# Weight conversion: low words rounded by ScalarE and added by GpSimd, the range test by TensorE, and new planner positions

## The chip, the cores and the metric

The kernel runs on one core of one Trainium2 chip. The metric is the device time of one execution in microseconds, the median of several runs. The core has five engines that run side by side, each working through its own queue in order: TensorE (PE in the profile, its weight loads PEld), VectorE (DVE), ScalarE (ACT), GpSimd (POOL) and SyncE (SP), which here issues nearly all DMAs.

## The reference

An attention block without softmax feeds a two-layer network:

```python
kv = np.einsum('bhsd,bhse->bhde', k, v)          # q, k, v: (8, 8, 576, 64) float32
out = np.einsum('bhsd,bhde->bhse', q, kv)
rms = np.sqrt(np.mean(out * out, axis=-1, keepdims=True) + 1e-06)
attn = (out / rms * g_norm).astype(np.float32)
x = attn.transpose(0, 2, 1, 3).reshape(4608, 512)
h = x @ w_in                                      # (512, 2048)
g = np.maximum(h, 0.0) + np.log1p(np.exp(-np.abs(h)))
return (g @ w_out).astype(np.float32)             # (2048, 512)
```

w_in and w_out are float64: every weight arrives as two 32-bit words, and the kernel makes a float32 of them before anything else.

## The kernel before

**Precision.** The large products run as three float32r matmuls each: an operand is split into a high part, a low part and a third part (high minus 4096 times low), in `split_weight` for weights and in `split` for x. Each split is a chain over ACT and DVE.

**Weights.** There are 16 chunks c of 128 of the 2048 inner columns. Operand j = 2c is the chunk of w_in, j = 2c + 1 that of w_out; each is 128 x 512 float64, 512 KB, fetched by SP into the buffer `raw` (`rawb` for odd j of the first eight chunks). Each of the two buffers has one place, so the next fetch into it waits for everything that reads the one before. `weight(j, ...)` then converts, for every operand:

- ACT `square` (L434) squares the exponent part of the high word, for a test of the weight's range;
- DVE `high1` (L438) and `high2` (L442) shift the bits of the high word, and the top three bits of the low word's share, into float32 form;
- DVE `mask` (L447) sets weights that are too small to zero;
- ACT `beyond` (L451) sums over the squares into a column of `over`, which shows weights that are too large; `whole_scale` adds up `over` late in the kernel and makes of it the factor `scale` of the last output stage;
- DVE `power` (L455) takes the weight's power of two, `rest` (L460) multiplies it with the low word, and `total` (L464) adds the two: the rounded float32.

The result goes into `split_weight`. For the first eight operands (chunks 0 to 3) the third part is made on PE, by two matmuls (L525, L526, `less_by_pe`); for the others on DVE.

**Attention.** Batch b needs its kv: five groups of matmuls (`kv_of`, L696), four of loads of 256 KB of k and of v and one of tails of 128 KB, then a copy by ACT (L704). Tile t is 128 rows of x. For a tile, q is loaded and turned (L776 on PE, copy L783, for the first tiles), then come `out_rows` (L720 on PE), the square by ACT (L793), its sum by DVE (L724), the root by GpSimd (L727, L728), the scaling by DVE (L732, `norm`), and for the first twelve tiles a turn by PE (L738), the split (ACT L640, DVE L643 and L646) and a copy and a store of x (L802, L803). Two tiles are under way at a time: the buffers for the squares, for the roots and for the rows in PSUM have two places each.

**The products.** Blocks of 384 rows (three tiles) take the chunks of their first part one by one: `mm1` (L864, twelve matmuls), softplus and split (ACT L886, L888, DVE L875, L879), and three `mm2` (L871, nine matmuls). Blocks 0 to 3 take chunks 0 to 3, the others chunks 0 to 5. The rest of the chunks runs in a wide stage over 512 rows with a scheme that saves products (L1066 and L1137), from 357 us on; x, and pieces of the result, go through DRAM in between.

**The order.** All operations are tasks with an engine, an assumed duration, what they follow, the buffers they take and give back, and a position. `Plan.order` builds the order of every queue before the program is emitted: on each engine it takes, among the tasks that could start about first, the one of the lowest position. The tables P0 to P7 hold the positions and offsets by position in the work; READY and BEGIN say from when an engine is assumed to be there. Where PE has nothing to do until the first products, the planner puts in fillers: matmuls of 128x512 whose result nobody reads (`warm`, L1237). The order is fixed in the program; on the chip an engine waits at the head of its queue.

Of the kernel before, what the change touches and what calls it, by code (L numbers as in the profile page):

```python
# [10 lines left out]
U32 = mybir.dt.uint32  # L11
BF16 = mybir.dt.bfloat16
# [48 lines left out]
class Plan:  # L61
# [5 lines left out]
    READY = {"PE": 2000, "ACT": 2500, "DVE": 4000, "POOL": 2500, "SP": 700}  # L67
# [4 lines left out]
    BEGIN = 2000  # L72
# [134 lines left out]
def kernel(  # L207
# [47 lines left out]
    P0 = [-45.94, -26.77, -11.8, 0.28, -29.91, -5.64, -2.86, 3.84, -103.4, -98.98, -69.3, -76.66, -68.5, -24.67, -23.22, -34.97, 8.15, -43.02, 7.47, 9.69, 7.18, 18.16, -12.1, 4.75, 1.0, 106.19, 31.3, 6.28, 7.19, 5.22]  # L255
    P4 = [-30.17, -6.08, 16.93, -33.9, -22.35, -28.91, -17.33, -7.12, -18.68, -2.69, 0.62, 2.73, -7.38, -1.86, 1.1, 1.72, 5.22, -13.65, 3.22, 0.88, 43.88, 43.95, -0.17, -0.32, 44.8, 40.82, -20.17, -6.56, 6.41, 10.03, -10.73, 0.23, 2.8, 0.42, -9.48, -5.03]
    P5 = [1.24, -5.69, -2.28, -3.57, 1.72, 0.53, 6.68, -5.83, 3.01, -2.95, 3.35, 1.4, -6.96, 0.27, -5.34, -2.29]
    P6 = [1.05, 6.24, 4.29, 4.08, -1.52, -2.85, 1.21, -0.34, 3.11, 3.1, -1.07, -0.73, -0.88, 9.99, 5.7, 5.69, 0.13, 0.46]
    P7 = [-23.78, -17.98, -11.85, -14.93, 0.41, 1.61, 7.35, 2.7, -25.02, -6.6, -15.2, -4.48, -2.14, 0.64, 2.93, 0.97, 4.67, 5.36, 3.33, 6.57, -10.37, 2.36, -14.11, -9.89, -7.11, 12.91, -2.89, 14.55, 12.59, 9.35]
    CONVERT, FETCH, EARLY, LATER = P0[:8], P0[8:16], P0[16:27], P0[27:]  # L260
    P1 = [49.11, 48.77, 51.0, 80.9, 122.61, 131.29, 2.87, 53.84, 71.21, 480.08, 304.47, 150.69]
    P2 = [24.08, 35.56, 23.68, 37.26, 50.08, 83.13, 74.26, 112.0, 102.25, 108.09, 139.38, -110.13, 88.34, 208.35, 423.47, -209.77, 170.15, -245.78, 423.49, 179.94, -7.53]
    P3 = [2.14, 2.48, 6.41, -16.53, 0.86, 2.79, 4.01, -16.44, 3.79, 3.96, 2.19, 1.79, 0.72, 1.35, 1.55, -1.03]
# [20 lines left out]
    big = const.tile([P, 1], F32, name="big")  # L284
    over = const.tile([P, 2 * KF], F32, name="over")
# [128 lines left out]
    def weight(j, pos, fetch_pos, behind):  # L414
# [12 lines left out]
        if wide:  # L427
            sq, t, p = (slot(n) for n in ("sq", "m", "m"))
# [25 lines left out]
            def power():  # L454
                nc.vector.tensor_scalar(out=new(p, [P, d_model], U32), in0=t.tile, scalar1=0xFF800000,  # L455
                                        scalar2=None, op0=ALU.bitwise_and)
# [816 lines left out]
```

## Time and profile before

| | |
|---|---|
| median of 3 runs | 858.36 us (858.07 to 860.5) |
| profiled execution | 858.36 us, its span 856.6 us |
| PE busy / span | 843.2 us, 98% |
| DVE, ACT, POOL busy | 704.3, 520.5, 76.0 us |
| granted TensorE clock | 1.00 |
| moved by DMA | 167.09 MB, 195 GB/s over the span |

How to read it: a busy PE is not a PE at its peak, since matmuls are pipelined and their ends are modelled; two matmuls in a row overlap in the records, so the time one takes is read from start to start. Idle time of an engine is put down to what came last before it went on. SPq is the queue of SP, the issue of DMAs. In a row like "L864 PE MATMUL banks<-units,pieces" stand the line, the engine, the operation, what is written and what is read.

### The profile page before, as it was taken

How to read it: one execution, taken by the hardware profiler on the slowest of the kernel's cores; microseconds unless marked ns; L12 is line 12 of the kernel's file. 1: busy time of each engine (PE TensorE's matmuls, PEld its weight loads, DVE VectorE, ACT ScalarE, POOL GpSimd, SP SyncE). 2: the span in 40 equal slices, each digit the busy share in tenths (PEclk: the TensorE clock that was granted, in tenths of full speed). 3: DMA queues.
4: the chain of work that ended last, by engine and by line, in shares of the span. 5: the costliest groups of instructions: out<-in, count | busy, mean ns of one | idle time of the engine just before them, and what ended most of it. 6: DMA issues, size and time to landing. Idle time of an engine off the chain costs nothing.

```text
span 856.6 us, 17087 instructions
## 1 busy us (share of the span) xinstructions
PE 843.2 (98%) x6469; PEld 754.6 (88%) x6469; DVE 704.3 (82%) x998; ACT 520.5 (61%) x980; POOL 76.0 (9%) x79
## 2 busy tenths in 40 slices
PE   8899999999999999999999999999999999999998
PEld 5578898999898999999999999998999899999996
DVE  7988898888788889798898788878788766788873
ACT  5866665446444567776667665655868555566654
POOL 0351223111113300000000000000000000000000
PEclk9999999999999999999999999999999999999999
DMA  9998997788774665436654546645364753787864
GB/s 277 284 237 225 268 262 239 180 245 221 216 180 120 185 172 187 139 111 205 212 155 152 186 149 204 197 158 181 123 196 140 233 167 102 240 240 242 250 190 130
DMA packets 239627, 167.09 MB, mean 195 GB/s; under 512 B 106168, under 2 KB 198584, under 8 KB 239544
## 3 DMA queue, kind: packets, MB, share of 16 engines
q1 hardware_dynamic: 239392, 165.86, 65.8%
q8 instruction: 51, 0.84, 0.4%
q14 instruction: 32, 0.26, 0.1%
q10 hardware_dynamic: 152, 0.13, 0.0%
HBM read 112.98 MB, written 52.95 MB: 194 GB/s over the span
## 4 chain that ended last, share of the span: by engine, by line
PE 94%; DMA 2%; DVE 1%; ACT 1%; POOL 0%; issue 0%; SPq 0%; ACTq 0%; DVEq 0%; POOLq 0%
PE banks L1137 31%; PE banks L1066 28%; PE banks L871 16%; PE banks L864 15%; PE banks L720 2%; PE banks L696 2%; DMA loads<-in_v_dram 1%; DMA loads<-in_k_dram 1%; PE banks L738 0%; DMA early<-in_g_norm_dram 0%; DVE half L732 0%; PE banks L1237 0%; PE banks L776 0%; POOL roots L728 0%; ACT half L793 0%
## 5 line engine op out<-in xcount | busy, mean ns | idle before, releaser
L1137 PE MATMUL banks<-pieces,gv 128*128 128x512 f32 x768 | 236.7, 390 | 0.0
L1137 PE MATMUL banks<-pieces,g_False 128*128 128x512 f32 x384 | 149.4, 389 | 0.0
L1137 PEld LDWEIGHTS banks<-pieces,gv 128*128 128x128 f32 x768 | 132.4, 188 | 17.2 <-DVE banks L910 0.2
L864 PE MATMUL banks<-units,pieces 128*128 128x384 f32 x768 | 144.8, 337 | 0.0
L871 PE MATMUL banks<-pieces,gv 128*128 128x512 f32 x576 | 143.3, 393 | 0.0
L864 PEld LDWEIGHTS banks<-units,pieces 128*128 128x128 f32 x768 | 134.7, 188 | 4.5
L871 PEld LDWEIGHTS banks<-pieces,gv 128*128 128x128 f32 x576 | 106.2, 188 | 19.0
L1066 PEld LDWEIGHTS banks<-units,pieces 128*128 128x128 f32 x840 | 111.0, 188 | 6.5 <-ACT banks L1112 0.4
L1066 PE MATMUL banks<-units,pieces 128*128 128x256 f32 x840 | 115.1, 280 | 0.0
L886 ACT ACTIVATE half<-banks 128x384 f32<-128x384 f32 x64 | 31.4, 491 | 96.0 <-PE banks L864 92.8
L1127 DVE TENSOR_TENSOR gv<-g_True,gv 128x1024 fp32r<-128x1024 f32 x47 | 57.5, 1223 | 35.9 <-ACT gv L1124 35.9
L1137 PEld LDWEIGHTS banks<-pieces,g_False 128*128 128x128 f32 x384 | 72.1, 188 | 15.1
L1066 PEld LDWEIGHTS banks<-units,w 128*128 128x128 f32 x504 | 66.7, 188 | 3.7 <-ACT banks L1112 0.2
L1066 PE MATMUL banks<-units,w 128*128 128x256 f32 x504 | 69.6, 280 | 0.0
L728 POOL TENSOR_TENSOR roots<-roots,half 128x8 f32<-128x8 f32 x36 | 62.2, 1728 | 3.0
L1130 DVE SCALAR_TENSOR_TENSOR g_False<-gv 128x1024 fp32r<-128x1024 f32 x47 | 57.5, 1224 | 1.5
L1029 DVE TENSOR_TENSOR units<-loads,units 128x1024 fp32r<-128x1024 f32 x42 | 51.2, 1218 | 6.0 <-ACT units L1026 5.9
L1094 ACT ACTIVATE g_True<-banks 128x256 f32<-128x256 f32 x96 | 36.7, 384 | 30.7 <-PE banks L1066 30.3
L1116 DVE TENSOR_TENSOR g_True<-banks,g_True 128x512 f32<-128x512 f32 x48 | 33.1, 690 | 25.5 <-PE banks L1066 19.5
L931 ACT ACTIVATE m<-banks 128x512 f32<-128x512 f32 x72 | 42.1, 595 | 18.2 <-PE banks L1137 12.5
L1032 DVE SCALAR_TENSOR_TENSOR units<-units 128x1024 fp32r<-128x1024 f32 x42 | 51.4, 1224 | 1.7
L1026 ACT ACTIVATE units<-loads 128x1024 fp32r<-128x1024 f32 x42 | 44.3, 1055 | 12.5 <-PE banks L1066 10.1
(118 smaller groups left out, 1249.3 us busy)
## 6 DMA issues: line engine op xcount, KB each, us to landing
loads<-x SPq DMA_DIRECT2D x180, 128.0 KB, 2.6
part<-m SPq DMA_DIRECT2D x72, 256.0 KB, 3.0
m<-part SPq DMA_DIRECT2D x72, 256.0 KB, 3.4
loads<-form SPq DMA_DIRECT2D x45, 256.0 KB, 3.4
form<-loads SPq DMA_DIRECT2D x36, 256.0 KB, 2.9
raw<-in_moe_w_in_dram SPq DMA_DIRECT2D x16, 512.0 KB, 4.4
loads<-in_k_dram SPq DMA_DIRECT2D x32, 256.0 KB, 4.3
loads<-in_v_dram SPq DMA_DIRECT2D x32, 256.0 KB, 4.6
```

The source lines that it names most:

```text
L728: nc.gpsimd.tensor_tensor(out=r.tile, in0=r.tile, in1=half, op=ALU.pow)
L864: nc.tensor.matmul(from_the_end(hp, w), lhsT=w_in.tile[:, i, kd * P:(kd + 1) * P], rhs=from_the_end(xv.tile[:, i, kd], w), start=(m == 0), ...
L871: nc.tensor.matmul(mine[i].tile, lhsT=gv.tile[:, m, i * P:(i + 1) * P], rhs=w_out.tile[:, m], start=(c == cs[0] and m == 0), stop=(c == cs ...
L931: a = add("ACT", 690 if ph == LAST else 600, lambda: nc.scalar.activation(new(ot, [P, d_model]), bank.tile, func=AF.Copy, scale=scale if p ...
L1026: nc.scalar.activation(part_of(0, F32R), xl.tile if m > 1 else xl.tile[:, 0], func=AF.Copy, scale=DOWN)
L1029: nc.vector.tensor_tensor(out=part_of(1, F32R), in0=xl.tile if m > 1 else xl.tile[:, 0], in1=part_of(0), op=ALU.subtract)
L1032: nc.vector.scalar_tensor_tensor(out=part_of(2, F32R), in0=part_of(1), scalar=-RADIX, in1=part_of(0), op0=ALU.mult, op1=ALU.add)
L1066: nc.tensor.matmul(from_the_end(place(q), (16, 8)[kd]), lhsT=w[:, m, at:at + P], rhs=from_the_end(dst.tile[:, m, v, kd] if u < 6 else dst. ...
L1094: nc.scalar.activation(dst, src, func=AF.Softplus, scale=1.0 + E)
L1127: nc.vector.tensor_tensor(out=gvt(1, F32R), in0=gt(), in1=gvt(0), op=ALU.subtract)
L1130: nc.vector.scalar_tensor_tensor(out=gt(F32R), in0=gvt(1), scalar=-RADIX, in1=gvt(0), op0=ALU.mult, op1=ALU.add)
L1137: nc.tensor.matmul(from_the_end(mine[i].tile, P), lhsT=(gvt(m, F32R) if m < 2 else gt(F32R))[:, c, i * P:(i + 1) * P], rhs=from_the_end(ou ...
```

## The change

In `weight`, the three DVE operations `power`, `rest` and `total` go. ScalarE reads the low word as an integer, scales it by 2^-29 and writes it as an integer (`rounded`): the value, 0 to 8, by which the bits of the high word must be raised. GpSimd adds the two as 32-bit integers in place (`total`). The result stays in the buffer of the high word, so an operand takes two places of the ring `m` instead of three.

For the first eight operands the sum of the squares goes to PE: four matmuls with one column each (`beyond_sums`) into a PSUM bank of the ring `h`, and a DVE operation over one column (`beyond_found`) writes it to `over`. The other 24 keep ACT's `beyond`.

READY of PE and BEGIN go from 2000 to 1500, and all positions P0 to P7 are new (left out in the diff), so the order of every queue is new.

```diff
-    READY = {"PE": 2000, "ACT": 2500, "DVE": 4000, "POOL": 2500, "SP": 700}
+    READY = {"PE": 1500, "ACT": 2500, "DVE": 4000, "POOL": 2500, "SP": 700}
...
-    BEGIN = 2000
+    BEGIN = 1500
...
+    small = const.tile([P, 2], BF16, name="small")[:, :1]
...
-            sq, t, p = (slot(n) for n in ("sq", "m", "m"))
+            sq, t, r = slot("sq"), w, slot("m")
...
-            def power():
-                nc.vector.tensor_scalar(out=new(p, [P, d_model], U32), in0=t.tile, scalar1=0xFF800000,
-                                        scalar2=None, op0=ALU.bitwise_and)
-
-            def rest():
-                pf = p.tile.bitcast(F32)
-                nc.vector.scalar_tensor_tensor(out=pf, in0=words_of()[0], scalar=2.0 ** -52, in1=pf,
-                                               op0=ALU.mult, op1=ALU.mult)
+            def beyond_sums():
+                y = new(found, [P, d_model])
+                for i in range(KD):
+                    nc.tensor.matmul(y[:, :1], lhsT=sq.tile[:, i * P:(i + 1) * P], rhs=small,
+                                     start=not i, stop=i == KD - 1)
+
+            def beyond_found():
+                nc.vector.tensor_scalar(out=over[:, j:j + 1], in0=found.tile[:, :1], scalar1=d_model * 2.0 ** 30,
+                                        scalar2=None, op0=ALU.add)
+
+            def rounded():
+                nc.scalar.activation(new(r, [P, d_model], I32), words_of()[0], func=AF.Copy, scale=2.0 ** -29)
 
             def total():
-                nc.vector.tensor_tensor(out=new(w, [P, d_model]), in0=t.tile.bitcast(F32),
-                                        in1=p.tile.bitcast(F32), op=ALU.add)
+                nc.gpsimd.tensor_tensor(out=t.tile.bitcast(I32), in0=t.tile.bitcast(I32),
+                                        in1=r.tile, op=ALU.add)
+                t.tile = t.tile.bitcast(F32)
 
             a1 = add("ACT", 670, square, [f], pos, [sq], [raw])
+            a2 = add("ACT", 670, rounded, [f], pos, [r], [raw])
             d1 = add("DVE", 430, high1, [f], pos, [t], [raw])
             d2 = add("DVE", 690, high2, [d1], pos, [], [raw])
             d3 = add("DVE", 690, mask, [d2, a1], pos, [])
-            over_done.append(add("ACT", 910, beyond, [d3], pos + (4 if c < 4 else 0), [], [sq]))
-            d4 = add("DVE", 430, power, [d3], pos, [p, w])
-            d5 = add("DVE", 690, rest, [d4], pos, [], [raw])
-            ready = add("DVE", 690, total, [d3, d5], pos, [], [t, p])
+            if c < 4:
+                d3.give.append(sq)
+                sq.readers += 1
+                found = slot("h")
+                b = add("PE", 310, beyond_sums, [a1], pos, [found], [sq])
+                over_done.append(add("DVE", 150, beyond_found, [b], pos, [], [found]))
+            else:
+                over_done.append(add("ACT", 910, beyond, [d3], pos, [], [sq]))
+            ready = add("POOL", 1200, total, [d3, a2], pos, [], [r])
...
-        a = add("DVE", 130, lambda: nc.vector.memset(new(ones, [P, P]), 1.0), (), pos, [ones])
+        a = add("DVE", 130, lambda: nc.vector.memset(new(ones, [P, P]), 1.0), over_done, pos, [ones])
...
+    nc.vector.memset(small, 2.0 ** -126)
```

What the two programs hold in their queues, counted in the orders as they were built (the first L864 is `mm1` of block 0 and chunk 0):

| | before | after |
|---|---|---|
| PE ahead of the first L864: groups of L696 / out_rows / turns of x | 10 / 6 / 4 | 10 / 6 / 4 |
| the same: turns of q / pairs L525, L526 / fillers / groups of beyond_sums | 9 / 5 / 55 / 0 | 8 / 6 / 39 / 7 |
| fillers in all | 57 | 39 |
| SP: operands fetched, in order | 0, 1, 2, 3, 4, 5, 6, (...) 7 | 0, 1, 2, 5, 4, 3, 6, (...) 8, 7 |
| SP: loaded ahead of the last load of batch 0's kv, with it | 4.75 MiB | 6.25 MiB |
| SP: the same for batch 1 | 10.0 MiB | 10.0 MiB |
| tiles split, in order | 0, 1, 3, 2, 4, 5 | 0, 1, 2, 3, 4, 5 |
| PE from the first to the fifth L864: L871 / L696 / out_rows / turns of x / turns of q / pairs / fillers | 27 / 5 / 5 / 5 / 1 / 2 / 1 | 27 / 2 / 3 / 4 / 2 / 1 / 0 |
| operands converted in the wide stage | 10 | 10 |

More of the change, by code (lines that the diff above doesn't have):

```diff
@@ L11 @@
 U32 = mybir.dt.uint32
+I32 = mybir.dt.int32
 BF16 = mybir.dt.bfloat16
@@ L258 @@
[L258 to L259 removed]
+    P0 = [-0.84, -4.22, -4.64, -4.59, -33.08, 1.26, -3.84, 4.91, -106.28, -63.71, -59.05, 73.29, -13.52, -55.66, -9.22, -6.37, -6.37, -43.36, 11.65, 10.14, 7.03, 23.99, -15.6, 4.21, 2.22, 37.72, -42.46, 0.58, 9.32, 5.06]
```

13 lines of the change are left out of this document (7 added, 6 removed).

## The prediction

> **What bounds the kernel now.** I read the page first.
>
> ```profile
> span 856.6 us, 17087 instructions
> ...
> PE 843.2 (98%) x6469; PEld 754.6 (88%) x6469; DVE 704.3 (82%) x998; ACT 520.5 (61%) x980; POOL 76.0 (9%) x79
> ...
> PE 94%; DMA 2%; DVE 1%; ACT 1%; POOL 0%; issue 0%; SPq 0%; ACTq 0%; DVEq 0%; POOLq 0%
> ```
>
> PE is busy for 98% of the span and makes up 94% of the chain that ended last; so the time is PE's dense work plus whatever PE loses at the start and behind the last matmul. The windows say where that is (columns: window, length, busy time of PE, PEld, DVE, ACT and POOL with instruction counts, clock, DMA share, GB/s).
>
> ```profile
> 0.00:10.00 10.00, 7.85 (x36) 5.78 (x36) 6.21 (x18) 4.06 (x6) 1.11 (x7) 1.00 0.86 258
> 10.00:20.00 10.00, 8.04 (x80) 5.60 (x81) 8.92 (x16) 7.41 (x15) 0.00 (x0) 1.00 1.05 309
> 20.00:30.00 10.00, 8.44 (x133) 6.03 (x129) 9.13 (x16) 8.28 (x19) 3.82 (x4) 1.00 0.95 268
> 30.00:40.00 10.00, 8.18 (x155) 6.22 (x154) 9.22 (x16) 8.73 (x18) 4.17 (x4) 1.00 1.08 291
> 40.00:50.00 10.00, 9.16 (x138) 7.46 (x137) 9.07 (x16) 6.25 (x13) 4.12 (x4) 1.00 1.08 242
> 50.00:60.00 10.00, 8.86 (x131) 7.41 (x130) 8.37 (x15) 8.41 (x17) 4.49 (x4) 1.00 0.93 224
> 420.00:440.00 20.00, 20.00 (x129) 18.13 (x128) 17.83 (x22) 13.56 (x27) 0.00 (x0) 1.00 0.66 209
> ```
>
> In the first 60 us PE is busy for 50.5 us and loses 9.5; the row of the wide stage (420 to 440) has 20.00 of 20.00. The clock is 1.00 throughout. The busy 50.5 us also hold fillers, matmuls with no result (L1237, 57 of them, below). DVE is at 8.9 to 9.2 of 10 from 10 to 50 us, and the DMA engines are full too (share 0.95 to 1.08). Three resources are tight at once in this stage, and the change relieves one of them.
>
> The chain of waits (start, us, what) and the timeline (start, us, engine, line, operation) show what the first L864, block 0 of the first product, waits for:
>
> ```profile
> 13.25 5.99 DMA loads<-in_k_dram
> ...
> 84.07 2.09 PE banks L864 x12
> 86.16 2.04 PE banks L871 x9
> ```
>
> ```profile
> 21.64 1.16 PE L720 MATMUL banks<-early,w 64*64 64x64 f32 x64
> ...
> 38.66 0.69 PE L696 MATMUL banks<-loads 128*64 128x64 f32 x16 [0.28 <-DMA loads<-in_v_dram]
> ...
> 40.40 0.69 DVE L646 SCALAR_TENSOR_TENSOR units<-units 128x512 fp32r<-128x512 f32 x1
> ...
> 42.28 0.69 PE L720 MATMUL banks<-early,w 64*64 64x64 f32 x32 [0.62 <-ACT half L793]
> ...
> 42.91 1.66 PE L1237 MATMUL banks<-ident_r 128*128 128x512 f32 x6
> ...
> 44.28 0.68 DVE L646 SCALAR_TENSOR_TENSOR units<-units 128x512 fp32r<-128x512 f32 x1
> ```
>
> The last load of batch 0's k and v was issued at 13.25 and took 5.99 us, so it landed at 19.24; the first out_rows (L720) ran at 21.64. The last loads of batch 1 let L696 run at 38.66. The third tile to be split was finished at 41.09 (40.40 + 0.69), the one that block 0 still lacked at 44.96; the six fillers at 42.91 held PE until the first L864 at 44.41. From there on:
>
> ```profile
> 44.41 2.25 PE L864 MATMUL banks<-units,pieces 128*128 128x384 f32 x12
> ...
> 49.20 0.66 PE L738 MATMUL banks<-ident_r,half 128*128 128x128 f32 x4
> ...
> 49.61 2.33 PE L864 MATMUL banks<-units,pieces 128*128 128x384 f32 x12
> ...
> 52.18 1.15 PE L696 MATMUL banks<-loads 128*64 128x64 f32 x32 [0.23 <-DVE units L643]
> 53.26 0.69 PE L720 MATMUL banks<-early,w 64*64 64x64 f32 x32
> 53.88 2.35 PE L864 MATMUL banks<-units,pieces 128*128 128x384 f32 x12
> ...
> 71.36 2.36 PE L864 MATMUL banks<-units,pieces 128*128 128x384 f32 x12
> ```
>
> The first L864 stands at 44.41, the fifth at 71.36: 26.95 us. By the chain an L864 group of twelve takes 2.09 and nine L871 matmuls 2.04; by successive starts two L696 groups take 1.08, one L720 group 0.62, one L738 group 0.41. From the first to the fifth PE did four L864 (8.4), 27 matmuls of L871 (6.1), five L696 (2.7), five L720 (3.1), five L738 (2.1), one L776 (0.4, the shape of L738), two L525/L526 pairs (about 1.2, as four matmuls of 128x512 of 0.23, and their turns): 24.0 us. So 3.0 us of this stretch are waits and turns.
>
> **The change part by part.** The rows for what goes and comes:
>
> ```profile
> L728 POOL TENSOR_TENSOR roots<-roots,half 128x8 f32<-128x8 f32 x36 | 62.2, 1728 | 3.0
> ...
> L451 ACT ACTIVATE sq<-sq,big 128x512 bf16<-128x512 bf16 x32 | 23.0, 717 | 9.2 <-DVE m L447 8.9
> ...
> L464 DVE TENSOR_TENSOR m<-m,m 128x512 f32<-128x512 f32 x32 | 22.0, 687 | 0.7
> ...
> L1237 PE MATMUL banks<-ident_r 128*128 128x512 f32 x57 | 19.5, 463 | 2.7 <-DVE ident_r L1195 1.6 <-ACT w L802 0.7 <-ACT pieces L529 0.2
> ...
> L460 DVE SCALAR_TENSOR_TENSOR m<-raw,m 128x512 f32<-128x512 uint32 x24 | 16.5, 686 | 0.5
> ...
> L434 ACT ACTIVATE sq<-raw 128x512 bf16<-128x512 bf16 x24 | 16.1, 671 | 0.9 <-DMA raw<-in_moe_w_in_dram 0.8
> ...
> L455 DVE TENSOR_SCALAR m<-m 128x512 uint32<-128x512 uint32 x32 | 13.6, 424 | 0.8
> ...
> L451 ACT ACTIVATION_READ_ACCUMULATOR sq<-sq,big 128x1 f32 x32 | 6.1, 190 | 0.0
> ...
> masks.py:199 POOL TENSOR_SCALAR_AFFINE_SELECT early<-early 128x128 f32<-128x128 f32 x1 | 0.3, 294 | 0.1
> ...
> L1181 PE MATMUL banks<-scale,m 128*128 128x1 f32 x2 | 0.3, 207 | 0.0
> ```
>
> *Off DVE:* power, rest and total, 0.424 + 0.686 + 0.687 = 1.80 us for each of 32 operands, 57.5 us in all. Eight operands are converted in the first 60 us (14.4 us), the other 24 later. There it buys nothing: PE is 20.00 of 20.00 busy with DVE at 17.83, and no PE wait is left to remove. Without that cover it would be up to 43 us.
>
> *Onto ACT:* rounded, 32 times the 0.671 us of L434 (same source, same size): 21.5 us; gone are eight beyond (0.717 + 0.190 = 0.91 us): 7.3 us. In the first 60 us ACT loses 1.9 us net and is at 4 to 8.7 of 10: priced at nothing. Its place is not free, though: rounded has to read the raw words before the next fetch may overwrite them, as rest did, and rounded of operand 4 stands ahead of the copy of batch 0's kv.
>
> *Onto PE:* 32 matmuls of one column, four for each of eight operands. L1181 is the nearest row, 0.207 us with a latency in it; four cost between 0.2 (pipelined) and 0.83 us, I take 0.3. Seven groups stand before the first L864, where 16 fillers fewer stand: hidden, and 2.1 us without those gaps. The eighth costs 0.3 us.
>
> *Onto GpSimd:* 32 integer adds of 128x512. No row has this. Below, DVE's add of that shape takes 0.687; above, one select over 128x128 took 0.294, four times as much for 512 and twice for the second operand is 2.35. I take 1.2, since the small row also holds a start-up. GpSimd is idle except for the roots, about 2 us a tile (1.728 for L728 and the 0.24 of a row below); an add ahead of a root delays it by up to 1.2.
>
> The Trainium skill, GPSIMD Engine Reference, section Elementwise — side-by-side cycle accounting, gives about 2.6 cycles an element for two operands, which I estimate at 1.1 us here; with it the sum is the same.
>
> *Smaller edits:* the fill of ones waits for over_done, far from any wait; the two planner constants change only the order; beyond_found is a one-column operation on DVE, between nothing and the 0.69 of a full one; even that is less than half of the 1.80 taken off for the same operand, which covers it.
>
> *The order.* That is where the gain has to come from, so I compared the issue orders of both programs. Before the first L864, both have the same real work on PE: ten L696 groups, six out_rows, four turns of x; ahead of the last load of batch 1 stand the same 10.0 MiB (seven operands, all k and v of two batches; seven tiles of q and one store of x, against eight of q). With the DMA engines full, this lands at about 38.7 in both, and out_rows of tiles 4 and 5 behind it stand ahead of the first L864 in both. The change cannot bring that L864 far below 42.
>
> Inside this, batch 0's last load now stands behind 6.25 MiB, not 4.75: 1.57 MB more, at 0.28 MB/us (between the rows with 309 and 268 GB/s) 5.6 us. First out_rows: 21.64 + 5.6 = 27.2. Before, three tiles took 19.45 us from there (to 41.09), and the window of this stretch for the line of rest alone (length, DVE busy and count) says how many operands DVE converted in it:
>
> ```profile
> 21.60:41.10 19.50, 2.07 (x3) 1.00 1.02 284
> ```
>
> Three, at 1.80 us each 5.4 at most; I count 3 of them on the chain. The third tile, which is now tile 2, the one block 0 needs, is then split at 27.2 + 16.5 = 43.7. An L864 can start some 0.7 us ahead of this, since the last third of its matmuls reads the third part; with out_rows and a turn before it I take 43.7, against 44.41: -0.7. The six fillers are gone, but the wait behind them was mostly real.
>
> Behind it, PE gets two L864 back to back. Up to the fifth it has four L864 (8.4), 27 matmuls of L871 (6.1), two L696 (1.1), three L720 (1.9), four L738 (1.6), two L776 (0.8), one pair (0.6): 20.5 us. Late next is the turn of tile 4, which waits for its root, 0.5 us by the same steps, and 0.5 more for turns: waits of 1.0 us instead of 3.0: -2.0.
>
> After that: a filler less (-0.3), 48 changes between tile shapes on PE instead of 52 (between 0 and one L871 matmul of 0.23 each, -0.9; I take -0.3), the eighth group of small matmuls (+0.3). In the wide stage the order of L1066 and L1137 differs, but between a product and the L1137 that waits for its result stands as much PE work as before, within one group of 0.7 us: 0. At the very end one L1137 group fewer covers the last split: between 0 and 0.7, I take 0.
>
> Sum: -0.7 - 2.0 - 0.3 - 0.3 + 0.3 = -3.0 us. The profiled execution took 858.36 (span 856.6 and 1.8 around it), which is the median of the three runs; so 855.4.
>
> **The rivals.**
>
> *A. The data decide.* If the DMA engines and the two slots for tiles set the pace, freeing DVE only moves idle time from DVE's queue to the loads: first L864 at 44.4, 3 us of waits behind it. For it: shares of 0.95 to 1.08, and batch 0 ready 5.6 us later. Against it: DVE at 9.1 in the same windows. Only the small terms remain: 858.4 - 0.3 = 858.1.
>
> *B. GpSimd's add holds DVE (slower).* Rows first:
>
> ```profile
> 36.39 0.68 DVE L447 SCALAR_TENSOR_TENSOR m<-sq,m 128x512 f32<-128x512 bf16 x1
> 36.56 0.61 POOL L727 TENSOR_SCALAR roots<-roots 128x8 f32<-128x8 f32 x1 [0.38 <-DVE roots L724]
> ...
> 34.20 0.24 POOL L727 TENSOR_SCALAR roots<-roots 128x8 f32<-128x8 f32 x1 [5.86 <-DVE roots L724]
> ```
>
> The 128x8 operation of GpSimd takes 0.24 us alone; begun within DVE's mask (two operands in SBUF) it took 0.61 and ended at 37.17, 0.10 after DVE. So the two share an access, and an operation that streams 512 elements can hold DVE as DVE held this one. One mechanism: each add follows a mask at once, and DVE's next operation mostly has two operands in SBUF. Held for all of 1.2 us, it gives back two thirds of what was taken away, and as a wait in the chain. In the start four of the adds (operands 4, 3, 6 and 8) lie on the way to the splits: +4.8 against the -3.0. Ten operands are converted in some twelve wide steps; if every third add stops PE for 1 us, 3 more. Time: 858.4 - 3.0 + 4.8 + 3 = 863; it turns the sign once about 3 us of such holds lie on the chain. Against it: the roots' second operation (1.7 us) overlaps DVE operations of unchanged length, but it reads eight elements only.
>
> The Trainium skill, SBUF — State Buffer, section Who interferes with whom, has this as a rule: the pair of ports is locked for a whole instruction and the other engine waits in full. The trace agrees that GpSimd waits for DVE; that DVE waits for GpSimd no row here shows.
>
> *C. The order's own idle closes.* The new order has 39 fillers for 57. At the row's 19.5/57 = 0.34 us, 18 fillers are 6.2 us; if all of it is time that PE no longer loses: 852.2. Against it stands the data bound at 42.
>
> **How the numbers follow.** Forecast 0.5 (own range 852.8 to 858), A 0.18, B 0.2, C 0.12. The time is the forecast's, 855.4. The range takes in C with a little to spare and most of B, where the add's price (0.7 to 2.35) is widest: 851 to 861.5. What a measurement can tell from no change is about 0.3%, 2.6 us, so the border is at 855.8: faster gets C and some 0.36 of the forecast's 0.5, same the rest and A, slower B and a little of A. Faster 0.48, same 0.30, slower 0.22.
>
> **What would show it.** Right: the first L864 near 43.7, the second directly behind it, the fifth at 64 to 67; DVE below 8 of 10 from 10 to 30 us; wide windows at 20.00 of 20.00. Wrong: an integer add far from 1.2 us; DVE operations with two operands in SBUF that take longer, or start late, beside an add (B); PE waits in the windows between 380 and 500 us; a load of batch 1 landing far from 38.7, or the first L864 under 41 (C). If the fifth L864 is still behind 69, A holds.

## The result, and the profile after

The changed kernel took 864.62 us (median of five, 862.17 to 867.01 in four of them) against 858.38 for the kernel before in the same session; the ratio, from those four, is 1.0063, interval 1.0034 to 1.0091. So it became slower by some 5.4 us, where 855.4 us and a range of 851 to 861.5 were forecast. The fifth execution, 1042.86 us, ran at a mean granted clock of 0.751 and happened to be the one profiled, so the profile shown here is of the same program run again (865.29 us, ratio 1.0070, interval 1.0058 to 1.0082; its own span 863.5).

First the page of the profile after.

```profile
span 863.5 us, 17104 instructions
...
PE 846.3 (98%) x6483; PEld 756.1 (88%) x6483; DVE 665.3 (77%) x911; ACT 531.4 (62%) x996; POOL 122.1 (14%) x111
...
PE 87%; DVE 4%; DMA 4%; ACT 2%; issue 1%; POOL 1%; SPq 1%; DVEq 0%; ACTq 0%
```

GpSimd's share rose from 9% to 14%, and PE has fallen from 94% to 87% of the chain that ended last. The windows of the start (window, length, busy time of PE, PEld, DVE, ACT and POOL with counts, clock, DMA share, GB/s) stand against those of before:

```profile
0.00:10.00 10.00, 7.03 (x26) 5.03 (x26) 3.70 (x14) 3.54 (x5) 2.32 (x8) 1.00 0.92 224
10.00:20.00 10.00, 7.60 (x77) 5.14 (x78) 5.96 (x10) 5.76 (x11) 3.10 (x2) 0.95 1.14 317
20.00:30.00 10.00, 9.25 (x97) 6.51 (x99) 5.26 (x10) 7.09 (x14) 2.53 (x2) 0.50 1.11 241
30.00:40.00 10.00, 8.39 (x158) 6.53 (x150) 7.33 (x13) 6.65 (x13) 5.07 (x5) 0.87 1.10 265
40.00:50.00 10.00, 7.78 (x145) 6.41 (x144) 7.80 (x14) 8.20 (x17) 5.71 (x6) 1.00 0.97 266
50.00:60.00 10.00, 9.65 (x83) 8.30 (x82) 8.63 (x15) 8.21 (x17) 6.03 (x6) 1.00 1.06 217
...
400.00:420.00 20.00, 19.96 (x123) 17.34 (x122) 18.06 (x20) 12.65 (x25) 3.08 (x2) 1.00 0.81 250
500.00:520.00 20.00, 19.90 (x129) 17.84 (x128) 14.95 (x20) 11.77 (x22) 1.61 (x1) 1.00 0.57 172
```

Three things can be read here. DVE came down as forecast, to 5.3 to 6 of 10 between 10 and 30 us. Between 10 and 40 us the DMA engines are busier than before (1.14, 1.11 and 1.10 for 1.05, 0.95 and 1.08), but from 20 us on they moved less: 241 GB/s between 20 and 30 us for 268, 265 for 291 in the next ten. And the clock granted to PE, 1.00 throughout before, is 0.50 between 20 and 30 us. In the wide stage the two windows shown are short of 20.00 by 0.04 and 0.10.

In the kernel after, most lines stand 13 further down: L696 is L709, L720 is L733, L738 is L751, L864 is L877 and L871 is L884. PE's timeline of the same run (start, us, engine, line, operation) says what became of the first block:

```profile
42.39 0.69 PE L709 MATMUL banks<-loads 128*64 128x64 f32 x16
42.91 0.64 PE L709 MATMUL banks<-g 128*64 128x64 f32 x16
44.19 0.63 PE L751 MATMUL banks<-ident_r,half 128*128 128x128 f32 x4 [0.64 <-ACT pieces L527]
...
46.11 0.69 PE L733 MATMUL banks<-early,w 64*64 64x64 f32 x32 [0.29 <-DVE half L745]
47.51 0.69 PE L733 MATMUL banks<-early,w 64*64 64x64 f32 x32 [0.71 <-ACT w L796]
48.13 0.66 PE L751 MATMUL banks<-ident_r,half 128*128 128x128 f32 x4
48.54 3.76 PE L877 MATMUL banks<-units,pieces 128*128 128x384 f32 x20
```

The last loads of batch 1 let L709 run at 42.39 and 42.91, where 38.7 was forecast; out_rows (L733) and the turn follow, and the first L877 stands at 48.54, where 43.7 was forecast and 44.41 was the time before. The last matmul ended the same 3.8 us ahead of the end of the span as before.

The new operations themselves cost about what they were priced at. First the line of the add (count, then the least, median and largest duration in ns), then the groups of lines (busy, mean ns of one):

```profile
L470 POOL TENSOR_TENSOR m<-m,m x32: 1262/1296/2374, 8.2 to 502.0; 128x512 int32<-128x512 int32 x32
```

```profile
L467 ACT ACTIVATE m<-raw 128x512 int32<-128x512 uint32 x24 | 16.1, 671 | 0.2 <-DMA raw<-in_moe_w_in_dram 0.2
...
L459 PE MATMUL banks<-small,sq 128*128 128x1 bf16 x32 | 2.0, 168 | 1.5 <-ACT sq L436 1.4
...
L463 DVE TENSOR_SCALAR over<-banks 128x1 f32<-128x1 f32 x8 | 1.1, 151 | 1.2 <-PE banks L459 1.2
```

An add takes 1.26 us at the least and 1.30 in the median (1.2 forecast), rounded 0.67 (0.671), a group of four one-column matmuls 0.25 (0.3), beyond_found 0.15.

### The profile page after: what moved, and what is told of

The parts are those of the page before. It is cut to its first block, busy times and chain, and to the rows that moved or that the text cites. A ratio compares the mean times of both kernels' runs of the same rounds, so it can differ in the third digit from the quotient of the medians.

```text
span 1041.1 us, 17104 instructions
## 1 busy us (share of the span) xinstructions
PE 1029.6 (99%) x6483; PEld 851.8 (82%) x6483; DVE 664.2 (64%) x911; ACT 531.9 (51%) x996; POOL 120.3 (12%) x111
## 4 chain that ended last, share of the span: by engine, by line
PE 96%; ACT 1%; DVE 1%; POOL 1%; DMA 0%; issue 0%; ACTq 0%; POOLq 0%; DVEq 0%
PE banks L1150 31%; PE banks L1079 27%; PE banks L884 16%; PE banks L877 16%; PE banks L733 2%; PE banks L709 2%; PE banks L751 1%; POOL m L470 0%; DMA early<-in_g_norm_dram 0%; POOL roots L741 0%; PE banks L789 0%; DVE m L449 0%; ACT sq L436 0%; ACT pieces L527 0%; ACT pieces L514 0%
## 5 line engine op out<-in xcount | busy, mean ns | idle before, releaser
L1150 PE MATMUL banks<-pieces,gv 128*128 128x512 f32 x696 | 257.2, 456 | 0.0
L884 PE MATMUL banks<-pieces,gv 128*128 128x512 f32 x576 | 176.6, 458 | 0.0
L877 PE MATMUL banks<-units,pieces 128*128 128x384 f32 x768 | 175.0, 387 | 0.0
L877 PEld LDWEIGHTS banks<-units,pieces 128*128 128x128 f32 x768 | 150.3, 200 | 20.7
L1150 PEld LDWEIGHTS banks<-pieces,gv 128*128 128x128 f32 x696 | 132.1, 203 | 37.2
L1150 PE MATMUL banks<-pieces,g_False 128*128 128x512 f32 x348 | 158.7, 456 | 0.0
L1079 PEld LDWEIGHTS banks<-units,pieces 128*128 128x128 f32 x948 | 145.7, 208 | 11.9
L1079 PE MATMUL banks<-units,pieces 128*128 128x256 f32 x948 | 152.2, 314 | 0.0
L884 PEld LDWEIGHTS banks<-pieces,gv 128*128 128x128 f32 x576 | 112.4, 198 | 39.3
L1140 DVE TENSOR_TENSOR gv<-g_True,gv 128x1024 fp32r<-128x1024 f32 x47 | 59.7, 1271 | 55.1 <-ACT gv L1137 55.1
L888 DVE TENSOR_TENSOR gv<-half,gv 128x384 fp32r<-128x384 f32 x64 | 36.7, 574 | 83.2 <-ACT gv L901 83.2
L470 POOL TENSOR_TENSOR m<-m,m 128x512 int32<-128x512 int32 x32 | 45.7, 1428 | 316.0 <-DVE m L449 200.8
L1079 PEld LDWEIGHTS banks<-units,w 128*128 128x128 f32 x396 | 62.0, 207 | 5.4 <-ACT g_True L1104 0.2
L741 POOL TENSOR_TENSOR roots<-roots,half 128x8 f32<-128x8 f32 x36 | 61.9, 1719 | 3.0
L1125 ACT COPY banks<-banks 128x256 f32<-128x256 f32 x48 | 17.4, 362 | 78.8 <-PE banks L1079 78.8
```

Source lines behind the costliest of these rows:

```text
L470: nc.gpsimd.tensor_tensor(out=t.tile.bitcast(I32), in0=t.tile.bitcast(I32), in1=r.tile, op=ALU.add)
L741: nc.gpsimd.tensor_tensor(out=r.tile, in0=r.tile, in1=half, op=ALU.pow)
L877: nc.tensor.matmul(from_the_end(hp, w), lhsT=w_in.tile[:, i, kd * P:(kd + 1) * P], rhs=from_the_end(xv.tile[:, i, kd], w), start=(m == 0), ...
L884: nc.tensor.matmul(mine[i].tile, lhsT=gv.tile[:, m, i * P:(i + 1) * P], rhs=w_out.tile[:, m], start=(c == cs[0] and m == 0), stop=(c == cs ...
L888: nc.vector.tensor_tensor(out=gv.tile[:, 1], in0=g.tile, in1=gv.tile.bitcast(F32)[:, 0], op=ALU.subtract)
L1079: nc.tensor.matmul(from_the_end(place(q), (16, 8)[kd]), lhsT=w[:, m, at:at + P], rhs=from_the_end(dst.tile[:, m, v, kd] if u < 6 else dst. ...
```

## The experiments

Theories, as they stood at first: **H**, GpSimd's add holds DVE (rival B of the prediction); **L**, the operand is merely ready later; **O**, the new order is worse. Ratios are to the kernel before in the same session.

**The add: left out, set aside, moved to DVE.**

```diff
 def total():                                # no_add: nothing issued
-    nc.gpsimd.tensor_tensor(out=t, in0=t, in1=r.tile, op=ALU.add)
+    nc.gpsimd.tensor_tensor(out=r.tile, in0=r.tile, in1=r.tile, op=ALU.add)   # add_aside
+    nc.vector.tensor_tensor(out=t, in0=t, in1=r.tile, op=ALU.add)             # add_dve
```

> The changed kernel once more, for a profile at full clock. All theories: 862 to 866 us (its four undisturbed times were 862.2 to 867.0). Theory H (GpSimd's add holds DVE): first L877 matmul near 46 to 48 us where 43.7 was forecast, DVE operations beside an add lasting 1.3 to 1.7 us where they take 0.69 alone. Theory L (the operand is late, DVE not held): DVE durations as before, but the splits begin 1.3 us behind each mask. Theory O (the order itself is worse): first L877 where it was forecast, and PE waits spread over the stages behind it.

> GpSimd's 32 integer adds are left out, so the low words are missing from the operands; every queue otherwise keeps its order. Theory H: the holds of DVE go, 4 x 1.2 in the start and about 3 us in the wide stage: 855 to 857 us. Theory L: the operand is ready 1.3 us sooner, the same 855 to 857. Theory O: the add was not what cost the time: 863 to 865.

> GpSimd's 32 adds stay at their places with their size, but add the rounded words to themselves, so nothing waits for them and the low words are missing from the operands. Theory H: DVE is held as in the changed kernel: 862 to 865 us. Theory L: nothing is late any more: 855 to 857, as without the adds. Theory O: 863 to 865, and the run without adds is no faster.

> The 32 integer adds are issued on DVE instead of GpSimd, at the same place of the order; DVE adds in float32, so the lowest bits of the operands are lost. Theory H: each add costs 0.69 us of DVE's queue where it cost a hold of 1.3: 859 to 861 us. Theory L: the operand is ready 0.6 us sooner: 859 to 861 too. Theory O: 863 to 865 or above, since DVE has more work in the same order.

Measured: without the adds 862.20 us, ratio 1.0047 (1.0035 to 1.0060); set aside 864.44, 1.0075 (1.0050 to 1.0100); on DVE 863.81, 1.0057 (1.0045 to 1.0069). An add for which nothing waits costs about as much as the real one; that speaks for H and against L, though the intervals of no_add and add_aside overlap a little, and a set-aside add still stands ahead of the roots in GpSimd's queue. The traces of inplace, below, show the hold itself. The adds are worth about 0.23% or 2 us here. But without them the kernel is still 4 us slower than before, and on DVE they miss the 859 to 861 us of H and L too. H is not the larger part.

**Too few fillers?** PE's clock in pieces of 3.41 us, the profile after:

```profile
12.13:15.54 3.41, 2.81 (x16) 1.56 (x14) 2.20 (x5) 3.08 (x6) 0.27 (x1) 1.00 1.11 342
15.54:18.96 3.42, 1.84 (x26) 1.52 (x26) 3.02 (x5) 1.24 (x3) 2.00 (x2) 1.00 1.16 314
18.96:22.37 3.41, 3.25 (x8) 1.73 (x6) 1.75 (x3) 2.91 (x6) 0.83 (x1) 0.50 1.20 211
22.37:25.78 3.41, 3.15 (x36) 2.39 (x37) 1.04 (x4) 2.56 (x6) 1.26 (x1) 0.50 1.24 260
25.78:29.20 3.42, 3.18 (x38) 2.21 (x34) 2.47 (x5) 1.65 (x4) 0.80 (x1) 0.50 0.99 213
29.20:32.61 3.41, 3.29 (x70) 3.10 (x71) 0.61 (x2) 1.75 (x4) 0.47 (x1) 0.50 0.99 319
32.61:36.02 3.41, 2.31 (x49) 1.64 (x51) 3.38 (x7) 3.06 (x6) 3.00 (x4) 1.00 1.23 257
```

PE was busy for 1.84 of 3.42 us, and from 18.96 on the clock is 0.50 for four such pieces, 13.65 us. With 39 fillers for 57 this suggested a theory **G**: the fillers that went kept the clock up. Against it **D**: the loads land late whatever PE does.

```diff
 def beyond_sums():                          # fill, fill_no_add: in the changed kernel
+    groups.append(j)
+    for i in range({2: 3, 3: 6, 4: 3, 5: 3, 6: 3}.get(len(groups), 0)):
+        nc.tensor.matmul(y, lhsT=ident_r, rhs=..., start=True, stop=True)
 def warm(s):                                # before_thin: in the kernel before
+    warmed.append(s)
+    if 22 < len(warmed) <= 40:
+        return
# old_pos: P0 to P7, READY and BEGIN of the kernel before, all else of the changed one
```

> 18 more fillers (128x512 matmuls without a result, 3 to 6 of them) stand ahead of the second to sixth group of one-column matmuls, in the stretch in which the profile of the changed kernel shows PE busy for only 1.84 of 3.41 us and then 13.65 us of half clock; all else keeps its order. Theory G (too few fillers, PE's clock falls): the granted clock stays at 1.00 and the time falls by 2 to 4 us, to 861 to 863. Theory D (the loads land late whatever PE does): the clock is restored but the first L877 group stays near 48 and the time at 864 to 866. Theory H (GpSimd's hold): 864 to 866 too.

> The same 18 fillers, and GpSimd's integer adds are left out, so the low words are missing from the operands. If G and H are two costs that add up: 858 to 860 us, about 2.5 below the run with fillers alone, as the adds cost before. If the adds cost only by letting PE fall idle and its clock with it: no more than 1 us below the run with fillers alone. Theory D: 862 to 864.

> The kernel before with 39 of its 57 fillers: the 18 that follow the first 22 (about 13 to 36 us) are not issued. They compute nothing that is used. Theory G: the granted clock falls to half for 3.4 us or more and the time rises to 860 to 863. If fillers only fill idle time and the clock does not matter: 858 to 859.

> The new conversion with the positions and planner constants of the kernel before. Theory O (the new positions are what costs): 857 to 860 us. If the new operations cost whatever their order (H, or ACT's and PE's added work): 863 us or more.

Measured: fill 866.70 us, 1.0079 (1.0060 to 1.0098), although its clock was nearly whole:

```profile
core 0: 865.6 us, clock 0.998
```

Its first L877 group stands at 48.81. fill_no_add took 864.35, 1.0050 (1.0035 to 1.0065). before_thin, with 6.8 us of half clock in its profile, took 860.05, 1.0002 (0.9991 to 1.0013). So G falls as the cause: fillers added and fillers taken away leave the time where it was. Going back to the old order is no cure: with the positions of before the new operations take 884.65 us (1.0287, 1.0272 to 1.0303). That the new order costs nothing by itself, and so that O falls, is shown only by inplace_no_add below.

**What the slow loads have in common.** D was left, and the DMA view has rows for it: packets, bytes and rate of the first 45 us, and the time that the queue's packets took as a share of 16 engines' time. First before, then after.

```profile
DMA packets 23877, 12.55 MB, mean 279 GB/s; under 512 B 15295, under 2 KB 23487, under 8 KB 23871
...
q1 hardware_dynamic: 23863, 12.47, 99.1%
```

```profile
DMA packets 20010, 11.73 MB, mean 261 GB/s; under 512 B 12070, under 2 KB 19622, under 8 KB 20006
...
q1 hardware_dynamic: 19998, 11.67, 105.1%
```

Less data (11.73 for 12.55 MB) took more engine time (105.1% for 99.1%). The trace has every packet's size and duration, and by size most of the difference lies in the 256-byte packets, which are the rows of q and of the tails of k and v: 18.3 ns before and 25.2 after in the mean. The 1,024-byte packets (k, v and w_in) went from 51.4 to 55.2 ns. An estimate from these means: 10,060 of the small packets at 6.9 ns more each are 69 us of engine time, or 4.3 us on each of 16 engines, and 6,126 of the larger ones at 3.8 ns add 1.5. The mean duration of the 256-byte packets over the first 40 us, for all eighteen profiles:

```
                    256-byte packets   first L864 or L877   tiles' place, bytes
before                   18.3 ns            44.41               0 mod 256
before_thin              18.1               46.39               0
before_shift256          18.0               47.08               0
inplace                  18.5               44.84               0
inplace_no_add           18.4               44.24               0
inplace_split4           18.2               47.93               0
before_shift             23.7               48.44              32
after                    25.2               48.54              32
no_add                   25.8               47.41              32
add_aside                27.3               50.89              32
add_dve                  26.7               48.21              32
fill                     25.6               48.81              32
fill_no_add              26.5               49.68              32
old_pos                  22.5               50.28              32
align                    25.2               48.47              64
align_no_add             24.0               46.76              64
align_old_pos            20.7               48.03              64
before_shift128          21.8               49.47             128
```

When the first nine of these (before, after and the seven runs so far) were there, old_pos had slow packets with the old order, and before_thin fast ones with a disturbed PE: so neither the order nor PE makes them slow, but something that every build of the new operations has. Such a thing is the new constant: small takes 32 bytes of each partition ahead of the big tiles, and all of them move. In the programs as built, the address of units, the first, goes from 17408, which is 68 times 256, to 17440. This is theory **S**.

```diff
-small = const.tile([P, 2], BF16, name="small")[:, :1]
+small = const.tile([P, 32], BF16, name="small")[:, :1]      # align, align_no_add, align_old_pos
+shift = const.tile([P, 1], F32, name="shift")               # before_shift: kernel before, next to big
+nc.vector.memset(shift, 0.0)
```

> The changed kernel with its new constant tile, small, taking 64 bytes a partition instead of 32, so that every tile allocated behind it starts at a multiple of 64 bytes again, as in the kernel before; no instruction and no order changes. Theory S (the 32-byte shift slows the loads of q, whose packets of 256 bytes took 18 ns before and 21 to 38 ns after): these packets at 18 ns again, the last loads of batch 1 landing near 39, the first L877 near 45 and the time at 857 to 861 us. Every other theory (clock, GpSimd's hold, the order): 863 to 866, as the changed kernel.

> The kernel before with an unused constant of one float (32 bytes a partition) ahead of the big tiles, written once by a memset, so that all big tiles start at 32 modulo 64 bytes; nothing else changes. Theory S: packets of 256 bytes at 21 to 38 ns in the first 50 us, the first L864 some 3 us later, 861 to 864 us. Every other theory: 858 to 859.5.

> As the aligned run, and without GpSimd's integer adds, so the low words are missing from the operands. Theory H beside S (the adds hold DVE, worth the 2.5 us that leaving them out saved without alignment): 2 to 3 us below the aligned run. If the adds then stand beside waits for data: within 1 us of it.

> The new conversion with the old positions took 884.65 us; here with the constant of 64 bytes. Theory S, if the shift was most of its loss of 25 us: 860 to 870 us. If the positions do not fit the new operations, whatever the alignment: 878 to 883.

Measured: before_shift 863.33 us, 1.0053 (1.0041 to 1.0065), with its first L864 4.03 us later than before:

```profile
48.44 0.86 PE L864 MATMUL banks<-units,pieces 128*128 128x384 f32 x4
```

An unused constant alone brings four of the lost microseconds into the kernel before. But align, with 64 bytes, still has slow packets (25.2 ns) and its first group at 48.47; at 863.00 us, 1.0044 (1.0031 to 1.0056), it gained some 2 us on the changed kernel, from where was not followed up. align_no_add took 861.65 (1.0033, 1.0020 to 1.0046), align_old_pos 881.96 (1.0271, 1.0252 to 1.0289). So the place matters, but multiples of 64 are not enough.

**Multiples of 256.** The addresses of the big tiles before are all multiples of 256.

```diff
+pair = const.tile([P, 2], F32, name="pair"); big = pair[:, :1]      # inplace, inplace_no_add
+small = pair[:, 1:].bitcast(BF16)[:, :1]                            # in big's unused bytes
+shift = const.tile([P, 64], F32, name="shift")                      # before_shift256; 32 for before_shift128
+nc.vector.memset(shift[:, :1], 0.0)
```

> The changed kernel with the new constant in the unused bytes behind the constant big (one tile of two floats for both), so that every big tile stands at its address of the kernel before, a multiple of 256 bytes; no instruction and no order changes. Theory S256 (tiles off the multiples of 256 bytes make the loads of q slow): packets of 256 bytes at 18 ns, the first L877 group near 44.5 instead of 48.5, the time 859 to 861 us, 4 below the changed kernel. If alignment is not it: 863 to 866.

> The kernel before with the same unused constant and the same memset as in the run with the shift of 32 bytes, but 256 bytes long, so that all big tiles stay at multiples of 256 bytes. Theory S256: 858 to 860 us, as the kernel before, the first L864 at 44 to 45. If the extra memset or tile costs, whatever the address: 862 to 864, as with 32 bytes.

> As the run with the constant in the unused bytes, and without GpSimd's integer adds, so the low words are missing from the operands. Theory H (the adds hold DVE on the chain): 2 to 3 us below that run, 856 to 858. If the adds are covered once the loads come in time: within 1 us of it.

Measured: inplace 861.48 us, 1.0029 (1.0012 to 1.0046); before_shift256, with the same memset as before_shift, 859.32, 0.9999 (0.9985 to 1.0012); inplace_no_add 858.75, 0.9992 (0.9979 to 1.0004). The packets are at 18 ns in all three, and inplace has the rate back in its first 45 us and its loads and first group nearly where they were forecast:

```profile
DMA packets 20738, 12.43 MB, mean 276 GB/s; under 512 B 12114, under 2 KB 20349, under 8 KB 20733
...
q1 hardware_dynamic: 20725, 12.37, 95.8%
```

```profile
39.37 0.69 PE L709 MATMUL banks<-loads 128*64 128x64 f32 x16 [0.77 <-DMA loads<-in_k_dram]
39.85 0.67 PE L709 MATMUL banks<-g 128*64 128x64 f32 x16
...
44.84 1.49 PE L877 MATMUL banks<-units,pieces 128*128 128x384 f32 x7
```

S256 is shown from both sides, by the packets and by the ratios: before_shift and before_shift256 differ in the length of the unused tile alone, and inplace and the changed kernel in the place of the constant. The time of inplace, 861.48, lies between the two forecast ranges, 0.5 us above that of S256. The profile of before_shift256 has its first L864 at 47.08 all the same: a half-clock stretch of 3.41 us stands at 33.7 in it, and before_thin has one of 6.83 us at 17.05. In these two profiles the first group came 2.7 and 2.0 us later than before with packets at 18 ns, and the medians did not follow (the profiled execution of before_shift256, 861.45 us, is the slowest of its twelve). I put this down to the half clock, which no run sets apart; so the first group of a single profile is no clean sign of the placement.

inplace and inplace_no_add issue the same matmuls in the same order, as do after and inplace, and before_shift and before; so each matmul can be set against itself. How much later it runs, in us, at points of the second trace:

```
at                      50      80     380     520     840 us
inplace - no adds      0.60    1.85    1.82    3.26    3.26
after - inplace        3.70    3.67    3.78    3.58    4.43
before_shift - before  4.04    4.04    4.60    4.60    4.92
```

The placement costs in the first 50 us. With the adds PE is 1.85 us later at 80 us. Of this 0.60 stands before the first product; the trace of inplace has 3.41 us of half clock at 16.64 and the other has none there, so that part is not shown to be the adds'. The other 1.25 come between 70 and 74 us. Another 1.44 come between 380 and 520, where the wide stage converts its operands. The chain behind the step at 70 us, timeline of inplace:

```profile
66.23 1.47 POOL L470 TENSOR_TENSOR m<-m,m 128x512 int32<-128x512 int32 x1 [2.20 <-ACT w L815]
66.66 1.46 DVE L892 SCALAR_TENSOR_TENSOR gv<-gv 128x384 fp32r<-128x384 f32 x1
68.04 0.67 DVE L737 TENSOR_REDUCE roots<-half 128x8 f32<-128x512 f32 x1
...
68.80 0.61 POOL L740 TENSOR_SCALAR roots<-roots 128x8 f32<-128x8 f32 x1 [1.10 <-DVE roots L737]
69.49 1.66 POOL L741 TENSOR_TENSOR roots<-roots,half 128x8 f32<-128x8 f32 x1
71.19 0.69 DVE L745 TENSOR_TENSOR half<-banks,roots 128x512 f32<-128x512 f32 x1 [1.88 <-POOL roots L741]
72.03 0.63 PE L751 MATMUL banks<-ident_r,half 128*128 128x128 f32 x4 [0.90 <-DVE half L745]
```

and the same operations without the adds:

```profile
66.06 0.56 DVE L892 SCALAR_TENSOR_TENSOR gv<-gv 128x384 fp32r<-128x384 f32 x1
66.54 0.68 DVE L737 TENSOR_REDUCE roots<-half 128x8 f32<-128x512 f32 x1
67.31 0.24 POOL L740 TENSOR_SCALAR roots<-roots 128x8 f32<-128x8 f32 x1 [3.87 <-DVE roots L737]
67.63 1.66 POOL L741 TENSOR_TENSOR roots<-roots,half 128x8 f32<-128x8 f32 x1
69.32 0.69 DVE L745 TENSOR_TENSOR half<-banks,roots 128x512 f32<-128x512 f32 x1 [0.72 <-POOL roots L741]
70.40 0.63 PE L751 MATMUL banks<-ident_r,half 128*128 128x128 f32 x4
```

L892 takes 0.56 alone; begun within the add it lasts to 68.12, 0.42 past the add's end (66.23 + 1.47). The reduction L737 is late by that, then GpSimd's root (L740, L741), then the product L745, and PE's turn L751 waits 0.90 us. GpSimd's own queue was not what was late: the add had ended at 67.70, and L740 began at 68.80, behind the reduction. In the wide stage larger operations are held:

```profile
498.37 1.61 POOL L470 TENSOR_TENSOR m<-m,m 128x512 int32<-128x512 int32 x1 [5.66 <-ACT m L467]
...
498.76 2.31 DVE L1140 TENSOR_TENSOR gv<-g_True,gv 128x1024 fp32r<-128x1024 f32 x1
```

L1140, 1.23 us alone, took 2.31. Between 380 and 500 us seven operations of DVE are held like this in that trace, and four of them stand 3 to 6 us ahead of a step in PE's lateness (at 402.67, 409.22, 467.31 and 502.98); the links between were not followed. Of DVE's operations that began beside an add, those with both operands in SBUF took up to 1.1 us longer (L1003 1.78 for 0.68, L888 1.66 for 0.56); those that read one operand from PSUM did not (L745, six times beside an add, 0.65 to 0.69). Of those with a single operand, in SBUF, the reduction L737 was not held (0.69 at most), but the shift L440, 0.42 us alone, was in the profile after, where it began 0.61 us before an add's end:

```profile
37.48 0.90 DVE L440 TENSOR_SCALAR m<-raw 128x512 uint32<-128x512 uint32 x1
```

The Trainium skill, SBUF — State Buffer, section Who interferes with whom, has the rule: the two engines share a pair of ports, an exclusive lock; a VectorE instruction with two SBUF inputs contends with a GpSimd instruction that reads SBUF, and one with at most one SBUF input does not, outside the modes that use two ports. The trace agrees for two inputs, for L745 and for L737, with the numbers above; whether L440 ran in such a mode it does not show.

**By instruction or by byte; 128 or 256.**

```diff
-nc.gpsimd.tensor_tensor(out=t, in0=t, in1=r.tile, op=ALU.add)
+for i in range(0, d_model, P):                                      # inplace_split4
+    nc.gpsimd.tensor_tensor(out=t[:, i:i + P], in0=t[:, i:i + P], in1=r.tile[:, i:i + P], op=ALU.add)
```

> As the run with the constant in the unused bytes, with each of GpSimd's 32 adds of 512 columns issued as four adds of 128 columns one behind the other. Theory H, by instruction (DVE waits until the running instruction of GpSimd ends): DVE operations beside adds last at most some 0.35 us longer instead of 1.1, the operand itself is ready a little later; 859 to 860.5 us, 1 to 2 below the run with whole adds. If the hold goes by the bytes moved: 861 to 862.5, no change.

> The kernel before with the unused constant and its memset, 128 bytes long: all big tiles at 128 modulo 256 bytes. If every place off the multiples of 256 bytes is slow for rows of 256 bytes: packets of 256 bytes at 21 ns or more, the first L864 2 to 4 us later, 861 to 864 us. If 128 is enough: 858 to 860.

Measured: inplace_split4 862.18 us, 1.0037 (1.0025 to 1.0049), no faster than inplace. The line of its adds (duration least, median, largest):

```profile
L471 POOL TENSOR_TENSOR m<-m,m x128: 447/462/1538, 7.8 to 503.3; 128x128 int32<-128x128 int32 x128
```

The hold does go by the instruction: DVE's operations beside a quarter add last at most 0.3 us longer (L1003 0.99, L1140 1.52). But four quarters take 1.85 us for 1.30, so the operand is ready later; the time was not won.

before_shift128: 861.07, 1.0020 (1.0003 to 1.0037), packets at 21.8 ns. Its twelve times go with PE's granted clock: 858.56 to 860.94 us in the six at 1.000, no more than the kernel before beside it (857.70 to 859.96 at 1.000), and 861.20 to 865.25 in the six below that. How much of the placement's price comes by way of PE's clock the runs do not separate: no execution of before_shift was at 1.000 (0.995 to 0.999), eleven of fourteen of the kernel before were. That slow loads cost time at full clock too is suggested by fill alone, two executions of which at 1.000 took 864.37 and 866.77 us, with 18 matmuls more.

No version here beats the kernel before: the best that computes everything, inplace, is 0.29% above it.

## Why the prediction was wrong

**The step that failed.** "With the DMA engines full, this lands at about 38.7 in both." The bytes ahead of the last load of batch 1 were compared, and the rate was taken over from before. The rate is what changed: 261 for 279 GB/s over the first 45 us, since the line that adds small moves every tile that a load writes. So L709 ran at 42.39 in place of 38.7. The text does not mention that line at all; it puts the new constant at nothing, without a reason. With the constant in unused bytes the last two L709 run at 39.37 and 39.85 (38.66 and 39.15 in the trace before) and the first L877 at 44.84. By the ratios, 1.0070 against 1.0029, the placement is worth 0.41%, 3.5 us.

**The add's hold.** This was the second step that failed: forecast at nothing, and as rival B at 4.8 us in the start and 3 in the wide stage. B's mechanism, DVE waiting for a whole add, is right. Its sizes were 1.25 us in the start, 1.85 at most, and 1.44 in the wide stage; and in the start the traced path is another, through a root behind L892 and not through the splits ahead of the first product. By the ratios the adds are worth 0.37%, 3.2 us, with the constant in place (1.0029 against 0.9992); the other three pairs with and without them, all with shifted tiles, give 0.11 to 0.29%. That B's 863 lies near the measured time is chance: it has more than twice the price for the adds, and nothing for the placement. The row that spoke for B, an operation of GpSimd stretched from 0.24 to 0.61 beside a DVE operation with two SBUF operands, showed GpSimd waiting for DVE; the reverse, which no row showed then, is what the runs showed.

**The gain.** With the constant in unused bytes and the adds left out (inplace_no_add) the ratio is 0.9992: 0.7 us, not told apart from nothing, for the 3.0 that were summed. So the gain was mis-sized too. The first L877 came at 44.24 (43.7 forecast). The fifth stood at 66.47, 65.2 by the sum; the order asks for 3.5 us less work between them than before (20.5 for 24.0), so of the 4.9 us by which it is earlier 1.4 are won, where 2.7 were forecast. About half of the 1.4 is lost again behind the fifth, where the sum followed no waits; one of them is that of PE's out_rows, 0.74 us at 113.4 in that trace. The others were not traced.

**What held.** The prices of single operations to 0.1 us, DVE below 8 of 10 up to 30 us, two L877 back to back, and nothing gained in the wide stage. Rival C falls: the fillers that went were not free time. With the placement and the adds taken out, what is left comes out near rival A: a ratio of 0.9992 against 0.9996 for its 858.1, the first group at 44.24 against 44.4, though the fifth at 66.47 is not behind 69.

## What to carry to other kernels

A tile allocated ahead of others moves them all: after adding a constant, compare the tiles' addresses modulo 256, and put small things into unused bytes or behind the big ones. When work goes to GpSimd, look which DVE operations with two SBUF operands will stand beside it, and price each with the whole of GpSimd's instruction. Two traces with the same order of matmuls, subtracted one from the other, show at which microsecond a loss arises; look first whether PE's clock was the same in both.

## What was not expected of the hardware

Loads with rows of 256 bytes into tiles 32, 64 or 128 bytes off a multiple of 256 took 20.7 to 27.3 ns a packet, against 18.0 to 18.5 on a multiple. The Trainium skill, DMA: Bandwidth & Descriptors, section How a descriptor splits into AXI transactions, has a rule that bears on it: when a descriptor does not start at a multiple of 256 bytes, its first transaction starts at the multiple below, and the bytes ahead of the start still cost beats. It speaks of reading; here it was the side written that moved. By its counts I estimate 9 beats for 8 for a row of 256 bytes at an offset of 32, an eighth more, and 12 at 128. The runs do not follow these counts: packets took a quarter to a half longer at 32 (22.5 to 27.3 ns for 18.3), and 21.8 ns at 128. So the mechanism stays open.

PE's half clock came in pieces: ahead of the last few microseconds of each profile, all its stretches in the eighteen lasted 3.41, 6.83 or 13.65 us, one, two or four times 3.413. Of the 27 stretches 25 follow a piece of that length in which PE was busy, as the records show it, for at most 0.58 of the time. The other two follow pieces at 0.60 and 0.75, and six pieces between 0.46 and 0.59 were followed by full clock, so no sharp limit comes out. A PE that is about half busy is thus not safe from it, and no long gap is needed.
